# A recurrence with a gated MLP: a chunk's scaled keys loaded as two transfers of 416 KB instead of one of 832 KB, under a new instruction order

## The chip, the cores and the metric

The kernel runs on one core of a Trainium2 chip. The metric is the device time of one execution in microseconds. Five engines take part: TensorE (PE) multiplies matrices, VectorE (DVE) and ScalarE (ACT) work on elements, GpSimd (POOL) only fills memory at the start, and SyncE (SP) issues the DMA transfers. Each engine runs its own list of instructions in order, and semaphores hold an instruction until what it needs is there.

## The reference

For 4 batches of 8 heads a state of 40 x 40 is carried over 768 time steps, and each step's output row goes through an MLP of 320 to 2048 to 320 features. All is float32.

```python
for t in range(S):                       # S = 768, D = 40
    y[:, :, t] = einsum('bhd,bhde->bhe', rt, state)
    Sa = einsum('bhde,bhe->bhd', state, at)
    state = state * wt[:, :, None, :] - einsum('bhd,bhe->bhde', Sa, bt) \
          + einsum('bhd,bhe->bhde', vt, kt)
x = y.transpose(0, 2, 1, 3).reshape(B * S, H * D)     # 3072 x 320
h = x @ w_in
sp = maximum(h, 0) + log1p(exp(-abs(h)))
out = (h * erf(sp)) @ w_out
```

## The kernel before

The 768 steps are cut into 12 segments of 64 steps (q), and each segment into two chunks of 32 steps (c = 0 and 1; c0 and c1 below), so there are 24 chunks. Within a chunk the steps are done at once by matrix products; from chunk to chunk the state MT is carried. For each segment the kernel does these stages:

- `prep` (L423): loads the decays of a segment (Pr, L429) and takes products along time by scans on DVE (L436, L440).
- `aphase` (L451), once per chunk: one DMA (L465) loads 104 x 2048 numbers, 832 KB, into one buffer `bk`. Its first half holds k and b (called bk), its second half a, laid out by diagonal blocks (called ab). DVE scales the second half (L466, "ab") and the first half (L468, "bk"). PE multiplies both (A, L473). Two DMAs copy the scaled ab to Zs (zs, L478). DVE masks A's result (Am, L484), and a DMA writes part of it to DRAM (AD, L486). PE transposes the scaled bk half (bT, L492). The buffer exists once, so the next chunk's load waits for all of these readers. In the very first segment c1 uses a part of the MLP's buffer (h) instead.
- `tphase` (L497), once per segment: DMAs bring A's blocks to Ti (L506) and Aw (L509), DVE solves 16 x 16 triangular blocks in 14 steps (L519, L520), DMAs write the result to DRAM (TD, L522) and read it back in another layout (Tb, L525), DVE transposes it (L528), and PE completes the inverse by two products (W and DAD, L538), with DVE adding the result (L545).
- `chain` (L547), once per chunk, in the order of the recurrence: the state is copied (zmm, L569), PE computes Z (L577) and U (L588), the rows of U are copied into Vu (zu, L598; four copies per chunk, each by ACT, DVE or an SP DMA), PE transposes (pmt L605, UT L614) and multiplies (PQ L624, MY L638 and L642), DVE updates the state (L645) and scales the outputs (L647). Its inputs are loaded by zv, vx, rt and rv (L559 to L564). At the end of a segment xw (L652) writes the rows to DRAM.
- The MLP of a segment: `load_x` (xr, L794), `mm1` (L816), the activation in `unit` (L831) and `post` (L854) with the second product (L877). Its matmuls have no part in the recurrence, so they fill PE between the small products of the chain. In the tables below an MLP group is one `mm1`, one `mm2` or one `mm2s` step, or one of the weight-preparation or warm-up products at the start.

The weights are loaded and split into two float32r parts in the first 130 us (`weights`, L706), beside 190 warm-up matmuls (L420).

All steps are put into a list with their readers and writers (`Plan.add`, L190). Two constants found by a search outside the kernel decide the order: `ORDER` (L15) lists the steps as they are emitted, and `ENGINES` has one letter per step for its engine (P, A, V, G, or S for a DMA issued by SP). `schedule` (L210) only reads them. Each engine runs its steps in that order. Every DMA of the program is issued by SP, in one queue.

Of the kernel before, what the change touches and what calls it, by code (L numbers as in the profile page):

```python
# [985 lines left out]
```

## Time and profile before

| what | value |
|---|---|
| median of 3 runs | 834.38 us (827.68 to 841.53) |
| profiled execution, its own time | 835.12 us |
| its span, first to last instruction | 833.3 us |
| PE, DVE, ACT busy | 729.1, 653.2, 539.4 us |
| mean granted clock of TensorE | 0.923 of full speed |
| bytes by DMA | 94.54 MB, mean 113 GB/s |
| loads of scaled keys | 24 of 832 KB each |

The span is the time from the program's first instruction to its last. Busy time of an engine leaves out waits and the issuing of DMAs. A name such as `bk<-in_kba_e` says that tile bk is written from tensor in_kba_e; `L466` is line 466 of the kernel. "issue" stands where the profile sees nothing that an engine waits for. PEld is PE's loading of weights, which runs beside its matmuls.

### The profile page before, as it was taken

To read this page: it belongs to the slowest core of one execution; us is meant where nothing else is said; L and a number is where in the kernel's file an instruction comes from. 1 tells how busy PE (TensorE), PEld (TensorE's weight loads), DVE (VectorE), ACT (ScalarE), POOL (GpSimd) and SP (SyncE) were. 2 spreads that over 40 slices of the span, in tenths; PEclk is the share of its full clock that TensorE was granted. 3 is DMA by queue.
4 is the path that set the end of the run, shared out by engine and by line. 5 is a ranking of instruction groups with operands and counts; after the bars stand their busy time and mean duration, and the time that the engine had idled before them with its cause. 6 is when DMAs were issued, how large, how long until landed. Compare 5 with 4: busy or idle time off the path is not lost.

```text
span 833.3 us, 31311 instructions
## 1 busy us (share of the span) xinstructions
PE 729.1 (87%) x13999; PEld 612.0 (73%) x13999; DVE 653.2 (78%) x1137; ACT 539.4 (65%) x759; POOL 4.1 (0%) x9
## 2 busy tenths in 40 slices
...
GB/s 188 217 246 148 139 185 86 89 125 134 147 105 113 124 80 113 124 105 134 160 43 133 169 62 93 151 60 109 153 78 101 115 95 124 96 74 52 32 16 20
DMA packets 173210, 94.54 MB, mean 113 GB/s; under 512 B 145708, under 2 KB 157356, under 8 KB 170572
## 3 DMA queue, kind: packets, MB, share of 16 engines
...
q8 instruction: 112, 1.84, 1.0%
...
## 4 chain that ended last, share of the span: by engine, by line
PE 43%; DVE 20%; DMA 16%; issue 11%; ACT 7%; SPq 3%; DVEq 0%; ACTq 0%
PE po L877 11%; PE ph L816 11%; PE pA L538 4%; PE my L638 3%; SPq L380 3%; PE pA L473 3%; PE my L588 2%; DMA vt<-in_rv_e 2%; PE pQ L624 2%; DVE tmp L519 2%; DVE Ti L520 2%; DMA Tb<-TD 2%; ACT r L824 2%; DMA h<-in_kba_e 2%; DMA xr<-xd 2%
## 5 line engine op out<-in xcount | busy, mean ns | idle before, releaser
L877 PE MATMUL po<-wo,h 128*128 128x320 f32 x384 | 131.0, 466 | 4.4 <-issue 3.6
L824 ACT ACTIVATE l<-l 128x1024 f32<-128x1024 f32 x96 | 99.2, 1056 | 16.4 <-DVE nd L847 15.8
L816 PE MATMUL ph<-xh,wih 128*128 128x256 f32 x384 | 92.3, 323 | 9.7 <-issue 6.6
L877 PEld LDWEIGHTS po<-wo,h 128*128 128x128 f32 x384 | 70.8, 202 | 22.3 <-issue 5.4
L816 PE MATMUL ph<-xh,wil 128*128 128x256 f32 x384 | 80.4, 292 | 0.0
L816 PE MATMUL ph<-xl,wih 128*128 128x256 f32 x384 | 80.3, 292 | 0.0
L816 PEld LDWEIGHTS ph<-xh,wih 128*128 128x128 f32 x384 | 64.3, 198 | 19.3 <-issue 8.3
L877 PE MATMUL po<-woh,gh 128*128 128x320 f32 x192 | 70.4, 367 | 0.4 <-ACT gh L374 0.3
L816 PEld LDWEIGHTS ph<-xh,wil 128*128 128x128 f32 x384 | 63.0, 201 | 2.8 <-issue 2.8
L877 PE MATMUL po<-woh,gl 128*128 128x320 f32 x192 | 61.6, 321 | 3.0 <-DVE gl L865 3.0
L374 ACT COPY Us<-my 128x320 f32<-128x320 f32 x23 | 9.8, 426 | 82.1 <-PE my L588 82.1
L816 PEld LDWEIGHTS ph<-xl,wih 128*128 128x128 f32 x384 | 62.8, 201 | 0.0
L816 PE MATMUL ph<-xl,wir 128*128 128x256 f32 x192 | 56.9, 296 | 5.3 <-issue 5.1
L877 PE MATMUL po<-wol,gh 128*128 128x320 f32 x192 | 61.2, 319 | 0.0
L847 DVE TENSOR_TENSOR nd<-l,r 128x1024 f32<-128x1024 f32 x48 | 58.4, 1216 | 2.5 <-ACT r L824 1.3
L858 DVE TENSOR_TENSOR l<-l,r 128x1024 f32<-128x1024 f32 x48 | 58.3, 1217 | 0.8 <-ACT l L824 0.4
L859 DVE SCALAR_TENSOR_TENSOR h<-l,h 128x1024 f32<-128x1024 f32 x48 | 58.4, 1219 | 0.6
L848 DVE SCALAR_TENSOR_TENSOR r<-nd,r 128x1024 f32<-128x1024 f32 x48 | 58.4, 1216 | 0.5
L816 PE MATMUL ph<-xh,wir 128*128 128x256 f32 x192 | 56.3, 293 | 0.3 <-DVE xh L376 0.2
L374 ACT COPY h<-ph 128x512 f32<-128x512 f32 x75 | 43.0, 582 | 17.5 <-PE ph L816 16.2
L638 PE MATMUL my<-Vu,sg 64*40 64x72 f32 x1536 | 47.5, 233 | 5.4 <-issue 1.3
L824 ACT ACTIVATE r<-l 128x1024 f32<-128x1024 f32 x48 | 49.3, 1053 | 4.4 <-DVE l L858 2.5
...
## 6 DMA issues: line engine op xcount, KB each, us to landing
...
Pr<-in_w_e SPq DMA_DIRECT2D x12, 422.9 KB
...
```

Of the source, the lines that this page charges most:

```text
L374: self.nc.scalar.copy(o, i)
L380: self.P.add(name, [("SP", ISSUE.get(name, 0.41))] + [("POOLQ", 1.0)] * (name in BULK), lambda e: q[e].dma_start(o(), i()), rd, wr, pr)
L473: nc.tensor.matmul(pa[i % 2 * 64:i % 2 * 64 + 64, i // 4, i // 2 % 2], bk[:, i].rearrange("p a b -> p (a b)"), ab[:, :, i], start=True, st ...
L538: nc.tensor.matmul(pw[js, i, ts], l[js, i], r[js, i, ts], start=True, stop=True)
L638: nc.tensor.matmul(my[h * 64:h * 64 + 40, x, j], sg[xs, g, j, h], vu[xs, g * HQ + j // 2 * 2 + h, j % 2], start=True, stop=False)
L816: nc.tensor.matmul(ph[:, j * 256:j * 256 + 256], a[:k, fs], b[:k], start=(m == 0), stop=(m == 7))
L824: self.P.add(name, "ACT", lambda e: nc.scalar.activation(out=o, in_=i, **kw), rd, wr + ["act"], pr, 1.06)
L847: P.add("nd", [("DVE", 1.2)], lambda e, r=r, l=l, nd=nd: s.eng(e).tensor_tensor(out=nd, in0=l, in1=r, op=ALU.mult), kl + kr, kn, pr)
L848: P.add("rho", "DVE", lambda e, r=r, nd=nd: nc.vector.scalar_tensor_tensor(out=r, in0=nd, scalar=2 * C4, in1=r, op0=ALU.add, op1=ALU.mult) ...
L858: P.add("E", [("DVE", 1.2)], lambda e: s.eng(e).tensor_tensor(out=l, in0=l, in1=r, op=ALU.mult), kr, kl, pr)
L859: P.add("G", "DVE", lambda e: nc.vector.scalar_tensor_tensor(out=h, in0=l, scalar=-1.0, in1=h, op0=ALU.add, op1=ALU.mult), kl, kh, pr, 1.2)
L877: nc.tensor.matmul(po, y[:, bs], w, start=(f == 0 and m == 0), stop=(f == 15 and m == len(ops) - 1))
```

## The change

The single load of a chunk becomes two: first the second half of the buffer (ab), whose readers are `ab`, A and zs, and then the first half (bk), whose readers are `bk`, A and bT. Each has its own dependences, so each can be issued when its own half is free. Bytes, multiplies and products are as before.

```diff
-        s.dma("kba", lambda: kb, lambda: s.I["kba_e"][ck], wr=kk + ka, pr=pr)
+        hw = 2 * NP * 32
+        s.dma("kba", lambda: kb[:, hw:], lambda: s.I["kba_e"][ck][:, hw:], wr=ka, pr=pr)
+        s.dma("kba", lambda: kb[:, :hw], lambda: s.I["kba_e"][ck][:, :hw], wr=kk, pr=pr)
```

`ORDER` and `ENGINES` are replaced as a whole (3720 steps instead of 3696). All five lists change. What the two constants say, counted:

| step | before | after |
|---|---|---|
| loads of scaled keys, by SP | 24 | 48 |
| zu: ACT / DVE / SP | 46 / 30 / 20 | 50 / 41 / 5 |
| zt: ACT / DVE | 21 / 3 | 16 / 8 |
| xh: ACT / DVE | 21 / 15 | 15 / 21 |
| ghi: ACT / DVE | 15 / 9 | 10 / 14 |
| hc: ACT / DVE | 75 / 21 | 80 / 16 |
| Wm: ACT / DVE | 8 / 4 | 10 / 2 |
| bTc, ysM, vtu, ob, wlo, ohi: ACT / DVE | 142 / 31 | 133 / 40 |
| MLP groups on PE between the last W and the first DAD | 42 | 26 |
| MLP groups between U and UT | 21 | 17 |
| MLP groups between UT and PQ | 20 | 15 |
| MLP groups between PQ and MY | 15 | 19 |
| next segment's c0 load in SP's list, 10 steady segments: before TD / between TD and tb / after tb | 3 / 0 / 7 loads | 13 / 5 / 2 halves |
| c1 halves that stand next to each other in SP's list | | 5 of 11 |

Four fills of the start (zmm's buffer, MT and two others) also change engine. SP's list of one steady segment, from the solve's input to the chain's loads, before and after (kba.ab and kba.bk are the halves):

```
Ti Ti out xr xr out zv vx xr xr w Ap rt Ap vx TD TD zv tb tb rv kba zs zs rv rv kba
Ti Ti Ap xr out xr out zs Ap xr xr w out kba.ab zv rv TD TD kba.bk tb tb rv vx zs zs vx rt out kba.ab rv rv kba.bk
```

## Rows read from the trace of the kernel before

**Rows 1.** Head of the page and busy time: us, share of the span, instructions.
```profile
span 833.3 us, 31311 instructions
...
PE 729.1 (87%) x13999; PEld 612.0 (73%) x13999; DVE 653.2 (78%) x1137; ACT 539.4 (65%) x759; POOL 4.1 (0%) x9
```

**Rows 2.** The chain that ended last: shares of the span by engine.
```profile
PE 43%; DVE 20%; DMA 16%; issue 11%; ACT 7%; SPq 3%; DVEq 0%; ACTq 0%
```

**Rows 3.** PE's waits: us in total, times, longest us.
```profile
PE my L588 <- issue: 17.2, 7, 4.0
PE ph L816 <- issue: 11.7, 4, 6.6
PE pA L538 <- issue: 9.0, 6, 3.0
PE my L577 <- issue: 7.6, 3, 5.1
PE pA L538 <- DVE Ti L528: 6.3, 5, 2.0
```

**Rows 4.** DMA queues: packets, MB, share of 16 engines' span.
```profile
q8 instruction: 112, 1.84, 1.0%
```

**Rows 5.** PE in order of time: start, us, what, idle before it.
```profile
82.39 0.87 PE L588 MATMUL my<-zt,Tb 32*32 32x40 f32 x37 [3.88 <-issue]
...
314.52 0.78 PE L577 MATMUL my<-Zm,Zs 96*32 96x40 f32 x62
320.37 0.29 PE L577 MATMUL my<-Zm,Zs 96*32 96x40 f32 x2 [5.07 <-issue]
...
632.91 0.94 PE L588 MATMUL my<-zt,Tb 32*32 32x40 f32 x51 [3.30 <-issue]
```

**Rows 6.** SP in order of time: a c1 load's issue.
```profile
311.29 0.34 SPq L380 DMA_DIRECT2D bk<-in_kba_e  x1
```

**Rows 7.** DMA queues in two stretches: 311 to 317 us, then 317.4 to 319.
```profile
q1 hardware_dynamic: 498, 1.17, 84.1%
...
q8 instruction: 1, 0.02, 5.6%
```

**Rows 8.** DVE's waits for the loads: us, times, longest.
```profile
DVE bk L466 <- DMA bk<-in_kba_e: 5.3, 4, 1.8
...
DVE bk L468 <- DMA bk<-in_kba_e: 4.5, 3, 2.7
```

**Rows 9.** Issues of the load by SP: ns min/median/max, first and last start.
```profile
L380 SPq DMA_DIRECT2D bk<-in_kba_e x23: 318/337/2345, 2.6 to 690.5; - x23
```

**Rows 10.** The chain in order of time: start, us, what (a DMA: issue to landing).
```profile
276.82 4.07 DMA Pr<-in_w_e
...
373.23 7.21 DMA bk<-in_kba_e
...
526.61 5.85 DMA Pr<-in_w_e
...
696.58 2.94 DMA Vu<-Us
```

**Rows 11.** SP in order of time around TD and Tb, in two segments.
```profile
349.37 1.13 SPq L380 DMA_DIRECT2D TD<-Ti  x2
...
352.35 1.35 SPq L380 DMA_DIRECT2D Tb<-TD  x2
...
399.97 0.34 SPq L380 DMA_DIRECT2D bk<-in_kba_e  x1
...
405.19 1.13 SPq L380 DMA_DIRECT2D TD<-Ti  x2
...
411.93 1.34 SPq L380 DMA_DIRECT2D Tb<-TD  x2
```

**Rows 12.** Copies of U's rows (L598) as instructions: ns min/median/max.
```profile
L598 ACT COPY Vu<-Us x46: 453/457/461, 66.7 to 760.7; 32x320 f32<-32x320 f32 x46
L598 DVE COPY Vu<-Us x30: 316/320/325, 69.4 to 742.4; 32x320 f32<-32x320 f32 x30
```

More of the change, by code (lines that the diff above doesn't have):

```diff
@@ L15 @@
 ORDER = tuple(int(x) for x in """
[117 rows of a table removed]
[117 rows of a table added]
 """.split())
 ENGINES = "".join("""
-SSVVGVGGVAVAGGVVVAAPPPPPPPPPPPPPPPPPPPPPPPPPPPPPPPPPPPPPPPPPPPPPPPPPPPPPPPPPPPPPPPPPPPPPPPPPPPPPPPPPPPPPPPPPPPPPPPPPPPPPPPPPPPPPPPPPPPPPPPPPPPPPPPPPPP
-PPPPPPPPPPPPPPPPPPPPPPPPPPPPPPPPPPPPPPPPPPPPPPPPPPPPPPPPPPPSAVVVVSVVPPSSVVSSPAPASVVPPSSVVSSPAPASSSSAAVVVVVVVVVVVVVVVVVVVVVVVVVVVVSSSSVPPPPAPPPPVSVVVAP
-APASVVVAPAPASVVVAAAPAAPAVSVVVAPVPASVVVAPAPASVVVAAAPAAPAASVVVAPAPASVVVAPAPVSVVVAPAPASVVVAPAPASVVVAVSVVVAVSVVVVVSVVVAVSVVVAVSVVVSVVVSVVVSVVVSVVVSAVVVVSV
@@ L138 @@
-VPPSSVVSSPAPASSSSSSVAPPAPPAVAVVPAPVPAPPVPVVPVVSVVPPSSVVSSPAPASSSSSSAAPPAPPAAAVVPAPAPAPPVPVVPVVSSSSSSSSSSSSAAVVVVVVVVVVVVVVVVVVVVVVVVVVVVSSSSVPPPPVPPPP
-VSAVSAVSSAVPPAPPAAPPAPPAAAAAAAAAAVVVVAAAPPAPPAAPPVPPVAVVAVPPPPPPPPVVPPPPPPPPSAVVVVSVVPPSSVVSSPVPASSSSSSVAAPPVPPAAVAAPAPAPAPPVPVVPVVSVVPPSSVVSSPAPASSSS
-SSVAPPAPPAAVVVPAPAPVPPVPVVPVVSSSSSSSSSSSSAAVVVVVVVVVVVVVVVVVVVVVVVVVVVVSSSSVPPPPAPPPPVSAVSAVSSAVAAAAAAAAVVVVAAAPPAPPAAPPAPPAAVVAVPPPPPPPPVVPPPPPPPPASS
-ASSAAAAAAAAVVVVAAAPPAPPAAPPAPPAAVVAVPPPPPPPPVVPPPPPPPPSAVVVVSVVPPSSVVSSPAPASSSSSSVAAPPAPPAVAAVPAPVPVPPVPVVPVVSVVPPSSVVSSPVPASSSSSSVAPPAPPVAVVAPAPAPAPP
@@ L142 @@
-VPVVPVVSSSSSSSSSSSSAAVVVVVVVVVVVVVVVVVVVVVVVVVVVVSSSSVPPPPAPPPPVSAVSAVSSVVAAAAAAAAVVVVAAAPPAPPAAPPAPPAAVVVVPPPPPPPPVVPPPPPPPPASSVSSAAAAAAAAVVVVAAAPPAP
-PAAPPAPPAAVVAVPPPPPPPPVVPPPPPPPPSAVVVVSVVPPSSVVSSPAPASSSSSSVAAPPAPPAAAVAPAPVPAPPVPVVPVVSVVPPSSVVSSPVPASSSSSSVVPPAPPAVVVVPAPAPAPPVPVVPVVSSSSSSSSSSSSAAV
-VVVVVVVVVVVVVVVVVVVVVVVVVVVSSSSVPPPPAPPPPVSAVSVVSSVVAAAAAAAAVVVVAAAPPVPPAAPPAPPAAVVVVPPPPPPPPVVPPPPPPPPASSASSAAAAAAAAVVVVAAAPPAPPVAPPAPPAAVVVVPPPPPPPP
-VVPPPPPPPPSAVVVVSVVPPSSVVSSPVPASSSSSSVVVPPAPPAAAAAPAPAPAPPVPVVPVVSVVPPSSVVSSPAPASSSSSSVVPPAPPAAASSPAPVPAPPVPVVPVVSSSSSSSSSSSSAAVVVVVVVVVVVVVVVVVVVVVVV
@@ L146 @@
-VVVVVSSSSVPPPPAPPPPVSVVSAVSSVVAAAAAAAAVVVVAAAPPVPPAAPPAPPAAVVAVPPPPPPPPVVPPPPPPPPASSASSAAAAAAAAVVVVAAAPPAPPAAPPAPPAAVVAVPPPPPPPPVVPPPPPPPPSAVVVVSVVPPS
-SVVSSPAPASSSSSSVAAPPAPPAVAAAPAPVPAPPVPVVPVVSVVPPSSVVSSPAPASSSSSSAVPPAPPAAVVVPAPVPAPPVPVVPVVSSSSSSSSSSSSAAVVVVVVVVVVVVVVVVVVVVVVVVVVVVSSSSVPPPPAPPPPVSV
-VSAVSSVVAAAAAAAAVVVVAAAPPAPPAAPPAPPAAVVVVPPPPPPPPVVPPPPPPPPASSASSAAAAAAAAVVVVAAAPPVPPAAPPAPPAAVVAVPPPPPPPPVVPPPPPPPPSAVVVVSVVPPSSVVSSPAPVSSSSSSVAAPPAP
-PASSAAPAPAPAPPVPVVPVVSVVPPSSVVSSPAPVSSSSSSVVPPAPPAASSAPAPAPAPPVPVVPVVSSSSSSSSSSSSAAVVVVVVVVVVVVVVVVVVVVVVVVVVVVSSSSVPPPPVPPPPVSVVSAVSSAVAAAAAAAAVVVVAA
@@ L150 @@
-APPVPPAAPPAPPVAVVAVPPPPPPPPVVPPPPPPPPASSASSAAAAAAAAVVVVAAAPPAPPVAPPAPPAAVVAVPPPPPPPPVVPPPPPPPPSAVVVVSVVPPSSVVSSPAPVSSSSSSVAAPPVPPAAAASPAPAPAPPVPVVPVVS
-VVPPSSVVSSPAPASSSSSSVAPPAPPAVSVSPVPVPAPPVPVVPVVSSSSSSSSSSSSAAVVVVVVVVVVVVVVVVVVVVVVVVVVVVSSSSVPPPPAPPPPVSVVSAVSSVVAAAAAAAAVVVVAAAPPAPPAAPPAPPAAVVAVPPP
-PPPPPVVPPPPPPPPASSASSAAAAAAAAVVVVAAAPPAPPVAPPAPPAAVVAVPPPPPPPPVVPPPPPPPPSAVVVVSVVPPSSVVSSPVPASSSSSSVAAPPAPPASAAVPAPAPAPPVPVVPVVSVVPPSSVVSSPAPASSSSSSVV
-PPAPPAVAAVPAPAPAPPVPVVPVVSSSSSSSSSSSSAAVVVVVVVVVVVVVVVVVVVVVVVVVVVVSSSSVPPPPVPPPPVSAVSAVSSAVAAAAAAAAVVVVAAAPPVPPAAPPAPPAAVVAVPPPPPPPPVVPPPPPPPPASSASSA
@@ L154 @@
-AAAAAAAVVVVAAAPPVPPVAPPAPPAAVVVVPPPPPPPPVVPPPPPPPPSAVVVVSVVPPSSVVSSPAPVSSSSSSVAAPPAPPASAAAPVPAPAPPVPVVPVVSVVPPSSVVSSPAPASSSSSSAVPPAPPASSVVPVPVPAPPVPVV
-PVVSSSSSSSSSSSSAAVVVVVVVVVVVVVVVVVVVVVVVVVVVVSSSSVPPPPAPPPPVSAVSAVSSVVAAAAAAAAVVVVAAAPPVPPAAPPAPPAAVVAVPPPPPPPPVVPPPPPPPPASSASSAAAAAAAAVVVVAAAPPAPPAAP
-PAPPAAVVAVPPPPPPPPVVPPPPPPPPSAVVVVSVVPPSSVVSSPAPASSSSSSVAAPPAPPASAASPAPAPAPPVPVVPVVSVVPPSSVVSSPAPVSSSSSSVAPPAPPAAASSPAPVPAPPVPVVPVVSSSSSSSSSSSSAAVVVVV
-VVVVVVVVVVVVVVVVVVVVVVVSSSSVPPPPVPPPPVSVVSAVSSVVAAAAAAAAVVVVAAAPPVPPAAPPAPPAAVVVVPPPPPPPPVVPPPPPPPPASSASSAAAAAAAAVVVVAAAPPAPPAAPPAPPAAVVVVPPPPPPPPVVPP
@@ L158 @@
-PPPPPPSSSSSSVAVPPVPPAVSSSPAPAPAPPVPVVPVVSSSSSSVVPPAPPAAAAAPAPAPAPPVPVVPVVSSSSSSSSVPVVSVVSAVSSVVAAAAAAAAVVVVAAAPPVPPAAPPAPPVAVVVVPPPPPPPPVVPPPPPPPPVSSV
-SSAAAAAAAAVVVVAAAPPVPPVAPPVPPVAVVVVPPPPPPPPVVPPPPPPPPAAAAAAAAVVVVAAAVVAVPPPPPPPPVVPPPPPPPPASSASS
+SSVVGVGAGVGGAGVVGAAPPPPPPPPPPPPPPPPPPPPPPPPPPPPPPPPPPPPPPPPPPPPPPPPPPPPPPPPPPPPPPPPPPPPPPPPPPPPPPPPPPPPPPPPPPPPPPPPPPPPPPPPPPPPPPPPPPPPPPPPPPPPPPPPPPP
+PPPPPPPPPPPPPPPPPPPPPPPPPPPPPPPPPPPPPPPPPPPPPPPPPPPPPPPPPPPSAVVVVSSVVPPSSVVSSPAPASSVVPPSSVVSSPAPVSSSSAAVVVVVVVVVVVVVVVVVVVVVVVVVVVVSSSSVPPPPAPPPPVSVVV
@@ new lines @@
+APAPASVVVAPAPASVVVAAAPAAPAASVVVAPVPASVVVAPAPASVVVAAAPVVPAVSVVVAPAPASVVVAPAPASVVVAPVPASVVVAPVPASVVVVVSVVVVVSVVVAVSVVVAVSVVVAVSVVVSVVVSVVVSVVVSVVVSAVVVV
+SSVVPPSSVVSSPAPASSSSSSVAPPAPPAVAVVPAPAPAPPVPVVPVVSSVVPPSSVVSSPAPASSSSSSAVPPAPPAVAAVPVPAPAPPVPVVPVVSSSSSSSSSSSSAAVVVVVVVVVVVVVVVVVVVVVVVVVVVVSSSSVPPPPA
+PPPPVSAVSAVSSVVPPAPPAAPPAPPAAAAAAAAAAVVVVAAAPPVPPAAPPAPPAAVVVVPPPPPPPPVVPPPPPPPPSAVVVVSSVVPPSSVVSSPAPASSSSSSVAAPPAPPAAAVAPAPVPAPPVPVVPVVSSVVPPSSVVSSPA
+PASSSSSSAVPPAPPAVVVVPAPAPVPPVPVVPVVSSSSSSSSSSSSAAVVVVVVVVVVVVVVVVVVVVVVVVVVVVSSSSVPPPPAPPPPVSAVSAVSSVVAAAAAAAAVVVVAAAPPAPPAAPPAPPAAVVAVPPPPPPPPVVPPPPP
@@ new lines @@
+PPPASSASSAAAAAAAAVVVVAAAPPAPPAAPPVPPAAVVAVPPPPPPPPVVPPPPPPPPSAVVVVSSVVPPSSVVSSPVPASSSSSSVAAPPAPPAVAVAPAPVPAPPVPVVPVVSSVVPPSSVVSSPAPASSSSSSAVPPAPPAAAAA
+PVPAPAPPVPVVPVVSSSSSSSSSSSSAAVVVVVVVVVVVVVVVVVVVVVVVVVVVVSSSSVPPPPVPPPPVSAVSAVSSVVAAAAAAAAVVVVAAAPPAPPVAPPAPPAAVVVVPPPPPPPPVVPPPPPPPPASSASSAAAAAAAAVVV
+VAAAPPAPPVAPPAPPAAVVAVPPPPPPPPVVPPPPPPPPSAVVVVSSVVPPSSVVSSPAPVSSSSSSVAAPPVPPAAVAVPAPVPAPPVPVVPVVSSVVPPSSVVSSPAPASSSSSSVAPPAPPAVVVVPAPAPAPPVPVVPVVSSSSS
+SSSSSSSAAVVVVVVVVVVVVVVVVVVVVVVVVVVVVSSSSVPPPPAPPPPVSAVSVVSSVVAAAAAAAAVVVVAAAPPVPPVAPPAPPAAVVVVPPPPPPPPVVPPPPPPPPASSASSAAAAAAAAVVVVAAAPPAPPAAPPAPPAAVV
@@ new lines @@
+AVPPPPPPPPVVPPPPPPPPSAVVVVSSVVPPSSVVSSPAPVSSSSSSVVAPPAPPAAAAAPAPAPAPPVPVVPVVSSVVPPSSVVSSPAPASSSSSSVVPPAPPAAVVVPAPAPAPPVPVVPVVSSSSSSSSSSSSAAVVVVVVVVVVV
+VVVVVVVVVVVVVVVVVSSSSVPPPPAPPPPVSVVSAVSSVVAAAAAAAAVVVVAAAPPVPPAAPPAPPAAVVAVPPPPPPPPVVPPPPPPPPASSASSAAAAAAAAVVVVAAAPPAPPAAPPAPPAAVVAVPPPPPPPPVVPPPPPPPP
+SAVVVVSSVVPPSSVVSSPVPVSSSSSSVVVPPAPPAVVAVPVPVPAPPVPVVPVVSSVVPPSSVVSSPAPASSSSSSAAPPVPPAAAASPVPAPAPPVPVVPVVSSSSSSSSSSSSAAVVVVVVVVVVVVVVVVVVVVVVVVVVVVSSS
+SVPPPPAPPPPVSVVSAVSSVVAAAAAAAAVVVVAAAPPAPPAAPPAPPAAVVVVPPPPPPPPVVPPPPPPPPASSASSAAAAAAAAVVVVAAAPPAPPAAPPAPPAAVVAVPPPPPPPPVVPPPPPPPPSAVVVVSSVVPPSSVVSSPV
@@ new lines @@
+PASSSSSSVVAPPAPPAAVAVPAPAPAPPVPVVPVVSSVVPPSSVVSSPAPASSSSSSVAPPAPPASAVAPVPAPAPPVPVVPVVSSSSSSSSSSSSAAVVVVVVVVVVVVVVVVVVVVVVVVVVVVSSSSVPPPPVPPPPVSVVSAVSS
+VVAAAAAAAAVVVVAAAPPAPPVAPPAPPAAVVVVPPPPPPPPVVPPPPPPPPASSVSSAAAAAAAAVVVVAAAPPAPPAAPPAPPAAVVVVPPPPPPPPVVPPPPPPPPSAVVVVSSVVPPSSVVSSPAPVSSSSSSVVAPPVPPAVVA
+APAPAPAPPVPVVPVVSSVVPPSSVVSSPAPASSSSSSVVPPVPPAAASAPAPAPAPPVPVVPVVSSSSSSSSSSSSAAVVVVVVVVVVVVVVVVVVVVVVVVVVVVSSSSVPPPPAPPPPVSAVSVVSSVVAAAAAAAAVVVVAAAPPA
+PPAAPPAPPAAVVVVPPPPPPPPVVPPPPPPPPASSASSAAAAAAAAVVVVAAAPPAPPAAPPAPPAAVVVVPPPPPPPPVVPPPPPPPPSAVVVVSSVVPPSSVVSSPVPASSSSSSVAAPPAPPAAVVAPAPVPAPPVPVVPVVSSVV
```

7 lines of the change are left out of this document (added), and 234 rows, old and new, of the table ORDER.

## Prediction

> **What bounds the kernel now.** I read the head of the profile, the chain that ended last, the waits of TensorE (PE), the DMA queues, and then single stretches in order of time. The head shows a span of 833.3 us with PE busy 729.1 us, VectorE (DVE) 653.2 and ScalarE (ACT) 539.4 [rows 1]: PE is the busiest and stands idle for 104.2 us. The chain lies on PE for 43% of the span and for 11% on "issue", waits whose cause the profile does not name [rows 2]. The waits of PE show where: four groups released by "issue" hold 17.2 + 11.7 + 9.0 + 7.6 = 45.5 us [rows 3], nearly half of its idle time.
>
> What that is, the queues tell. Queue q8 carries 112 blocks of instructions, 1.84 MB [rows 4]; PE runs 2 x 13999 instructions [rows 1], so about 250 to a block (an estimate by division). In the stretch 310 to 324 us PE stops two matmuls before the end of a run of Z and goes on after 5.07 us [rows 5]. The load of a chunk's scaled keys, 832 KB, was issued at 311.3 us [rows 6]. From 311 to 317 us the one program queue q1 moves 498 packets and q8 none; from 317.4 to 319 us q8's block comes [rows 7], and PE resumes at 320.37. So PE runs out of code, and the next block stands behind the big load. Ten waits of PE of over 2 us ended by "issue" begin within 9 us of such a load's issue. By the time at which PE resumes they are 82.39 (3.88 us), 139.78 (4.54), 254.22 (2.27), 296.64 (6.63), 320.37 (5.07), 481.29 (2.69), 504.62 (3.30), 545.48 (2.33), 571.65 (3.96) and 632.91 (3.30), 38.0 us in all; the first, the fifth and the last are shown [rows 5]. Seven of the ten follow the load of a segment's second chunk (c1, 26.3 us), three that of a first chunk (c0, 11.7 us). DVE itself waits for these loads only 5.3 + 4.5 us [rows 8].
>
> **The change, part by part.** *Two halves instead of one load.* The multiplies, matmuls and copies stay; 24 issues become 48. An issue holds SP for 0.337 us [rows 9], so 8.1 us are added. Fifteen of the 20 copies of U rows (zu) that SP issued go to DVE (11) and ACT (4), so SP nets nothing; its spare time hides the rest. Each half has its own wait: the a·P half (ab) for the matmul A and the zs copies that read it, the k,b half (bk) for the transposes bT. Behind a half that waits stand TD, tb, zs and rv on SP, and the solve's matmuls W and the Z and PQ of the chain wait for those.
>
> *Code held behind the load.* A load of 832 KB takes 7.21 us from issue to landing. The nearest row for 416 KB is Pr, 422.9 KB in as many rows: 4.07 and 5.85 us [rows 10]. A block of code can so be held 1.4 to 3.1 us less; between ends not far apart I take the middle, 2.25. For c1, seven waits, each longer than that: 7 x 2.25 = 15.8 us. Ends: 0, if both halves hold code like one load (5 of the 11 c1 pairs stand next to each other in SP's list), and 21.1 with 3.1 each (the 2.27 wait cannot give more). The Trainium skill, DMA: Bandwidth & Descriptors, section "Queues, rings and completion order", says that a DMA engine takes turns between queue rows packet by packet; by that adjacent halves, too, hold a block for one half only, and the sum would stay 15.8 without the end at 0. That a block comes while a big load's packets are done and later ones still flow [rows 7] agrees, but no row shows two loads together.
>
> *The c0 load moves.* In the steady segments the old order issued 3 of 10 c0 loads before TD (the solve's write), 7 after tb (its read-back). The new list has 13 of 20 halves before TD, 5 between TD and tb, 2 after. Before TD, PE runs MLP matmuls, and none of the three old loads there (one stands in [rows 11]) is followed by a wait for code within 9 us. I take 13/20 of the c0 waits as gone: 11.7 x 13/20 = 7.6 us; ends 0 and 11.7.
>
> Together 23.4 us of PE's idle time. How much reaches the end? The chain runs over PE and its issue waits for 43% + 11% [rows 2]; where PE is released earlier elsewhere, DVE (78% busy) or a DMA is late next. I take 0.55: 12.9 us; ends 0 and 32.8 (21.1 + 11.7, all of it).
>
> *The solve's round trip.* This is what the move costs. Normally TD's issue to Tb's takes 352.35 - 349.37 = 2.98 us; in the segment where the load went out 5.2 us before TD it took 411.93 - 405.19 = 6.74 [rows 11], 3.76 more. For five halves between TD and tb I take half of that, 1.9 us, and that it shows in 5 of 12 segments, since W already waits for the transposed block Ti five times in 12 segments [rows 3]: 5 x 1.9 x 5/12 = 4.0 us lost. Ends 0 and 18.8.
>
> *zu off SP.* One such copy by DMA lies on the chain with 2.94 us [rows 10]; as an instruction it takes 0.32 on DVE or 0.457 on ACT [rows 12]. One of the fifteen on the path gains 2.5 us, which I take; ends -3.5 (11 x 0.32 on DVE, none on the path) and 15 x 2.5 = 37.5, far too much, as the chain shows one. DVE has 180 us free to hide the new copies; without that cover they cost the 3.5.
>
> *The rest of the order.* PE's list has the same instructions. MLP groups between W and DAD fall from 42 to 26 (12 segments), between U and UT from 21 to 17, UT and PQ from 20 to 15; between PQ and MY they rise from 15 to 19. Some 30 other small instructions change between ACT and DVE both ways, under DVE's spare time. PE's idle time beside the four groups is 58.7 us; I take 0, ends 10 us (a sixth of that) either way.
>
> The sum: 12.9 + 2.5 - 4.0 = 11.4 us. The profiled execution took 835.1 us (span and 1.8 us around it), 0.7 above the median of the runs, 834.4. 835.1 - 11.4 - 0.7 = 823.0.
>
> **Rivals.** *Code is held as before* (the halves stand in the rings as one load; what is gained at one block is lost at another, as 112 blocks meet 48 loads). For it: rv pairs and other loads stand around the c1 load. Against: c0 loads before TD left no wait. Only zu and the round trip remain: 834.4 - 2.5 + 4.0 = 836. The Trainium skill, Runtime: NRT & Kernel Launch, section "Instruction fetch mechanics", calls the cost of a block boundary mostly hidden; by that there would be nothing to gain, and the time is this rival's. The waits of 3 to 6 us here [rows 5] disagree; the measurement decides.
>
> *Slower: the round trip becomes the bound.* Loads before and between TD and tb make Tb late in all ten steady segments by the whole 3.76 us of [rows 11], 37.6 us. It decides from the point where the MLP groups ahead of W are used up, so that PE waits for Ti each time. Less the gains above (15.4): 834.4 + 37.6 - 15.4 = 857. For it: 18 of 20 halves are now ahead of tb. Against: in 7 of 12 segments W does not wait for Ti today, and a half is in flight a shorter time.
>
> *Much faster: code waits behind key loads vanish.* If a block held by a half always comes before PE's stored code ends, all 38.0 us go, and reach the end, with zu's 2.5: 834.4 - 40.5 = 794; with the round trip's price 798. For it: waits of 2.3 to 3.3 us (five of ten) are about as long as what a half saves. Against: DVE and ACT then bound stretches.
>
> **How the numbers follow.** Forecast 0.48 (own range 812 to 834: half the way to each term's end, added in squares), code held as before 0.22, slower 0.12, much faster 0.18. Two per cent is about what a measurement of this kernel tells from no change: below 817.7 or above 851.1. Faster: nearly all of the last case (0.17), a third of the forecast (0.16) and a hundredth of the second, 0.34; slower: 0.10 of the slower case and 0.02 from elsewhere, 0.12; within, 0.54. The range takes in part of both outer cases: 802 to 842.
>
> **What would show it.** Right: issue waits of PE over 2 us within 9 us of a key load fall from 38.0 to about 15 us, none longer than 4.5; PE busy stays near 729; two issues per chunk on SP; TD to Tb around 3 to 5 us. The code part is wrong if those waits still sum to over 30 us; the round-trip term if Tb follows TD by 6 us in most segments and W's wait for Ti is above 20 us in total; the order if PE's idle time grows outside both.

## The result, and the profile after

The changed kernel takes 785.29 us (median of 4 runs, 782.47 to 789.87), the kernel before 837.95 in the runs beside it (4 runs, 827.68 to 842.34): a ratio of 0.9455 [0.9353, 0.9557], faster by 5.5%. Medians are of all runs and ratios of the runs near each kernel's fastest, so a ratio is not the quotient of two medians. The forecast was 823.0 with a range of 802 to 842; the time lies outside the range and below even the rival called much faster (794).

The head of the page of the changed kernel, busy time, and the shares of its chain, as in [rows 1, 2]:

```profile
span 780.7 us, 31363 instructions
...
PE 710.6 (91%) x13999; PEld 597.3 (77%) x13999; DVE 658.7 (84%) x1164; ACT 534.7 (68%) x748; POOL 4.6 (1%) x11
...
PE 52%; DVE 28%; issue 7%; ACT 6%; DMA 5%; SPq 1%; DVEq 0%; ACTq 0%
```

The span is 52.6 us shorter, and that comes in two pieces. PE's idle time (span less busy) falls from 104.2 to 70.1 us, by 34.1. PE's busy time falls from 729.1 to 710.6, by 18.5, with the same 13999 matmuls. On the chain, DMA falls from 16% to 5% and issue from 11% to 7%; PE and DVE take their place.

PE's waits that "issue" ended (lines after the load stand two further down: L588 of [rows 3] is L590, L816 is L818, L538 is L540, L577 is L579):

```profile
PE pA L540 <- issue: 10.3, 13, 1.8
PE my L579 <- issue: 3.2, 3, 2.8
PE ph L818 <- issue: 3.1, 2, 2.0
PE pA L540 <- DVE Ti L530: 1.9, 4, 0.9
PE my L590 <- issue: 0.7, 2, 0.5
```

The four groups of [rows 3] held 45.5 us; they hold 17.3. The one that remains, at L540, is 13 short waits, none over 1.8 us (9.0 us before, 10.3 now). The wait of the solve's matmul for Ti (DVE) fell from 6.3 to 1.9. Added up over the trace, PE's waits over 0.25 us that "issue" ended and that begin within 9 us of the issue of a key load ("near waits" from here on) were 41.4 us before and are 10.4 now. Of the ten over 2 us, 38.0 us in all, one of 2.80 is left. VectorE (DVE) waited 12.1 us for the key loads (the two groups of [rows 8] and 2.3 us for the first tile's load); now no wait of DVE is ended by one.

How a block of code comes through is seen in the queues, two stretches of the changed kernel around a c1 pair whose halves were issued at 290.89 and 295.84 us: first 290.9 to 294.7, then 294.5 to 296.

```profile
q1 hardware_dynamic: 617, 0.49, 46.7%
...
q1 hardware_dynamic: 87, 0.01, 5.6%
q8 instruction: 1, 0.02, 4.2%
```

In the first stretch q1 moves 0.49 MB, the first half among it, and q8 nothing; in the second q1 is nearly empty and q8's block comes (294.78 to 295.79), just before the second half is issued. PE does not wait for this block. The block of [rows 7] came when 93 of the load's 104 packets had ended. The chain shows the length of one half, issue to landing (start, us, what):

```profile
582.03 3.63 DMA bk<-in_kba_e
```

That is 3.63 us against 7.21 for the whole load [rows 10]. These are single rows: over all loads, from the issue to the end of the last packet, the median is 6.7 us for the 24 whole loads before and 3.9 us for the 48 halves.

The issues themselves cost what [rows 9] said (ns min/median/max), and a Tb behind a half that was issued between TD and Tb comes 4.36 us after TD (SP in order of time, as [rows 11]):

```profile
L380 SPq DMA_DIRECT2D bk<-in_kba_e x46: 308/338/1732, 1.3 to 642.9; - x46
```

```profile
328.49 1.15 SPq L380 DMA_DIRECT2D TD<-Ti  x2
329.73 0.51 SPq L380 DMA_DIRECT2D bk<-in_kba_e  x1
332.85 1.36 SPq L380 DMA_DIRECT2D Tb<-TD  x2
```

**Where the busy time went.** The page's costliest group did the same 384 matmuls in less time, first before, then after (busy us, mean ns of one):

```profile
L877 PE MATMUL po<-wo,h 128*128 128x320 f32 x384 | 131.0, 466 | 4.4 <-issue 3.6
```

```profile
L879 PE MATMUL po<-wo,h 128*128 128x320 f32 x384 | 124.6, 446 | 0.2 <-DVE h L861 0.2
```

The mean granted clock was 0.923 before and is 0.959 after. Windows of the kernel before around the fifth wait of [rows 5] show when it falls (us, busy of PE, PEld, DVE, ACT, POOL, then PEclk, DMA share, GB/s):

```profile
300.00:315.30 15.30, 15.11 (x495) 12.81 (x495) 11.26 (x16) 8.64 (x14) 0.00 (x0) 0.93 0.27 64
315.30:320.40 5.10, 0.03 (x2) 0.03 (x1) 1.42 (x2) 0.00 (x0) 0.00 (x0) 0.88 0.86 185
320.40:326.10 5.70, 5.70 (x83) 4.98 (x82) 3.09 (x4) 3.14 (x6) 0.00 (x0) 0.51 0.16 29
326.10:340.00 13.90, 13.86 (x251) 11.96 (x251) 12.33 (x16) 9.55 (x13) 0.00 (x0) 1.00 0.46 111
```

PE waits 5.07 us for its code, and the 5.70 us of work behind it run at 0.51, which is the 1.2 GHz level; then the clock is back at 2.4 GHz. So this wait is paid twice. Time at the lower level was 130.5 us before and is 66.4 after. All ten waits of the prediction, and an eleventh of 1.81 us near a key load, have such a stretch that begins inside the wait or within 1 us of its end. These eleven stretches are 81.9 of the 130.5 us; in the changed kernel 3.4 of the 66.4 us stand so behind a near wait, and the other 63.0 do not.

### The profile page after: what moved, and what is told of

The parts are those of the page before. It is cut to its first block, busy times and chain, and to the rows that moved or that the text cites. A ratio compares the mean times of both kernels' runs of the same rounds, so it can differ in the third digit from the quotient of the medians.

```text
span 780.7 us, 31363 instructions
## 1 busy us (share of the span) xinstructions
PE 710.6 (91%) x13999; PEld 597.3 (77%) x13999; DVE 658.7 (84%) x1164; ACT 534.7 (68%) x748; POOL 4.6 (1%) x11
## 4 chain that ended last, share of the span: by engine, by line
PE 52%; DVE 28%; issue 7%; ACT 6%; DMA 5%; SPq 1%; DVEq 0%; ACTq 0%
PE ph L818 14%; PE po L879 13%; PE ph L420 5%; PE pA L540 4%; PE my L640 3%; DVE Zs L486 2%; DVE h L861 2%; PE pA L475 2%; DVE l L860 2%; DVE r L850 2%; DMA TD<-Ti 2%; DVE Ti L522 2%; DVE gl L867 2%; DVE tmp L521 2%; DMA Tb<-TD 2%
## 5 line engine op out<-in xcount | busy, mean ns | idle before, releaser
L879 PE MATMUL po<-wo,h 128*128 128x320 f32 x384 | 124.6, 446 | 0.2 <-DVE h L861 0.2
L818 PE MATMUL ph<-xh,wih 128*128 128x256 f32 x384 | 92.1, 321 | 1.1 <-issue 1.1
L818 PE MATMUL ph<-xl,wih 128*128 128x256 f32 x384 | 79.9, 290 | 2.3 <-issue 2.0
L879 PEld LDWEIGHTS po<-wo,h 128*128 128x128 f32 x384 | 67.5, 192 | 16.6 <-DVE h L861 0.5
L818 PE MATMUL ph<-xh,wil 128*128 128x256 f32 x384 | 79.4, 290 | 0.0
L879 PE MATMUL po<-woh,gh 128*128 128x320 f32 x192 | 73.1, 380 | 4.4 <-DVE ob L376 3.7
L818 PEld LDWEIGHTS ph<-xh,wih 128*128 128x128 f32 x384 | 63.3, 195 | 6.8
L374 ACT COPY h<-ph 128x512 f32<-128x512 f32 x80 | 46.7, 584 | 30.6 <-PE ph L818 24.9
L818 PEld LDWEIGHTS ph<-xl,wih 128*128 128x128 f32 x384 | 61.8, 198 | 2.7 <-issue 2.3
L818 PEld LDWEIGHTS ph<-xh,wil 128*128 128x128 f32 x384 | 62.2, 199 | 0.0
L818 PE MATMUL ph<-xh,wir 128*128 128x256 f32 x192 | 55.6, 289 | 2.6 <-DVE xh L376 2.6
L640 PEld LDWEIGHTS my<-Vu,sg 64*40 64x40 f32 x1536 | 36.4, 117 | 26.2 <-DVE Vu L629 10.9
L818 PE MATMUL ph<-xl,wir 128*128 128x256 f32 x192 | 55.8, 291 | 0.1
L420 PE MATMUL ph<-d 104*128 104x512 bf16 x190 | 50.4, 405 | 1.6 <-DVE d L391 1.6
```

The source lines that it names most:

```text
L374: self.nc.scalar.copy(o, i)
L420: P.add("warm", "PE", lambda e: nc.tensor.matmul(s.ph[1], s.d1[:, :128], s.d1[:, :512], start=True, stop=True), ["d1"], ["phw"], -1e3, 0.22)
L640: nc.tensor.matmul(my[h * 64:h * 64 + 40, x, j], sg[xs, g, j, h], vu[xs, g * HQ + j // 2 * 2 + h, j % 2], start=True, stop=False)
L818: nc.tensor.matmul(ph[:, j * 256:j * 256 + 256], a[:k, fs], b[:k], start=(m == 0), stop=(m == 7))
L879: nc.tensor.matmul(po, y[:, bs], w, start=(f == 0 and m == 0), stop=(f == 15 and m == len(ops) - 1))
```

## The experiments

Each ratio is to the kernel before in runs on the same chip. "Old order" and "changed order" name the lists of steps and engines of the two kernels.

**1. Halves or order?** Three kernels complete a table. Old order, the halves next to each other where the one load stood:

```diff
-s.dma("kba", lambda: kb, lambda: s.I["kba_e"][ck], wr=kk + ka, pr=pr)
+s.dma("kba", lambda: kb[:, hw:], lambda: s.I["kba_e"][ck][:, hw:], wr=ka, pr=pr)
+s.dma("kba", lambda: kb[:, :hw], lambda: s.I["kba_e"][ck][:, :hw], wr=kk, pr=pr)
 ORDER: each load's number becomes two, next to each other
```

> The order and engines of the kernel before, with each load cut into its two halves, issued next to each other where the one load stood. Theory H (blocks of code are held behind a key load, a half holds them for half as long, adjacent halves let a block in between): waits of PE on issue within 9 us of a key load fall from 41 us to 10 to 18, the granted clock rises above 0.94, time 795 to 815 us. Theory O (the gain is the new order's; loads are placed and products covered better): waits on issue stay near 40 us, time 830 to 840 us.

Changed order, one load, at the place of the later half; four ab multiplies that would come before it move behind it:

```diff
-s.dma("kba", lambda: kb[:, hw:], lambda: s.I["kba_e"][ck][:, hw:], wr=ka, pr=pr)
-s.dma("kba", lambda: kb[:, :hw], lambda: s.I["kba_e"][ck][:, :hw], wr=kk, pr=pr)
+s.dma("kba", lambda: kb, lambda: s.I["kba_e"][ck], wr=kk + ka, pr=pr)
```

> The new order and engines, but one load of 832 KB, at the place of the later of its two halves (four multiplies of ab move behind it). Theory H: waits on issue within 9 us of a key load come back to 25 to 40 us, clock near 0.93, time 815 to 835 us. Theory O: time 785 to 800 us, waits on issue below 15 us.

Changed order, both halves next to each other at that same place:

```diff
 ORDER, every chunk
-ab half, other steps, bk half
+other steps, ab half, bk half
```

> The changed kernel with both halves of a load issued next to each other, at the place of the later one; the same as the new order with one load (841 us) except that the load is in two. Theory H (a half holds code for half as long wherever it stands): 785 to 800 us, waits on issue near loads 10 to 20 us. Theory P (the earlier place of the first half matters, not the halving): 825 to 845 us, waits on issue near loads over 30 us.

Measured: old order in halves 811.17 us, 0.9743 [0.9645, 0.984]; changed order with one load 840.92, 1.0127 [1.0033, 1.0221]; with adjacent halves 818.21, 0.9809 [0.9737, 0.9881]. So halving in place gives 2.6% in the old order and 3.1% in the new, and the new order with one load gives nothing, or costs a little. The rest of the 5.5%, from 0.9809 to 0.9455, comes with the earlier place of the first half. What the order costs with one load is seen in DVE's waits for it, 32.2 us, with single waits over 6 us:

```profile
DVE bk L466 <- DMA bk<-in_kba_e: 19.6, 9, 6.3
...
DVE bk L468 <- DMA bk<-in_kba_e: 12.6, 3, 7.6
```

**2. Which chunk's early half?** Changed kernel, adjacent halves for the first chunks (c0) only, then for the second chunks (c1) only:

```diff
 ORDER, every first chunk
-ab half, other steps, bk half
+other steps, ab half, bk half
```

> Changed kernel (785 us), but the two halves of every first chunk (c0) are issued together, at the place of the later one; the second chunk's (c1) stay apart. With both chunks together it took 818 us, so 33 us are to be shared out. If the early half counts by the prediction's terms (c1 15.8, c0 7.6), about two thirds of the 33 us stay: 796 us (790 to 802), with the waits over 2 us near key loads at 8 to 10 us (4.8 with both apart, 17.2 with both together). If c0's early half is what counts, because DVE multiplies sooner and the transfers of TD are not behind 832 KB: 808 to 818 us. If a single early half is worth nothing without the other: 812 to 820 us.

```diff
 ORDER, every second chunk
-ab half, other steps, bk half
+other steps, ab half, bk half
```

> Changed kernel, but the two halves of every second chunk (c1) are issued together, at the place of the later one, with the few multiplies that then come too early moved behind; the first chunk's (c0) stay apart. By the prediction's terms c1 carries two thirds of the 33 us: 807 us (800 to 812), waits over 2 us near key loads 12 to 15 us. If c0's early half is what counts: 787 to 796 us. If neither is worth anything alone: 812 to 820 us.

(The 4.8 and 17.2 us in these texts count every issue wait over 2 us; in the changed kernel one of its two, of 2.05 us, begins 9.6 us after a load.) Measured: c0 together 804.76 us, 0.9682 [0.9622, 0.9742]; c1 together 790.38, 0.9528 [0.951, 0.9547]. These times stand beside other runs of the kernel before than those of e7 and of the changed kernel, so the ratios are to be compared: 0.9809 with both together, 0.9455 with both apart. C1's early halves alone bring 1.3% (some 11 us), and their interval touches that of both together; c0's alone bring 2.8% (some 23 us), and their interval lies inside that of the changed kernel. So c0's early half carries most of it, and no share of c1's is clear of noise. The traces agree: near waits are 20.7 us with c0 together and 9.6 with c1 together. Two lines of the kernel with c0 together, PE's wait and DVE's, show the largest part:

```profile
PE pA L540 <- issue: 18.9, 12, 7.2
```

```profile
DVE bk L470 <- DMA bk<-in_kba_e: 12.9, 2, 6.8
```

The 7.2 and the 6.8 us stand behind one c0 pair, issued 4.4 and 6.0 us after TD; the other wait of DVE, 6.1 us, is for the program's first loads.

**3. The copies of U rows.** Changed kernel with the engines of these copies (zu) as before, 20 on SP; old order with 18 of the 20 taken off SP, in one load and in halves; changed kernel with the last five on DVE:

```diff
 ENGINES, zu
-5 S
+20 S
```

> The changed kernel, with only the engines of the copies of U's rows (zu) as before: 20 of them by SP again instead of 5. The prediction's term: 2.5 us lost, so 787 to 789 us. If each of the fifteen lay on the path: up to 822 us. If the copies had no part: 783 to 787 us.

```diff
 ENGINES, zu, old order, one load
-20 S
+2 S, 7 more V, 11 more A
```

> The kernel before, one load and the old order, with 18 of the 20 copies of U's rows (zu) that SP issued given to the engines that the changed kernel uses (DVE 7, ACT 11). Theory Q (a zu issue at the head of SP's queue waits for U, and holds every transfer behind it): PE's waits other than issue fall by 10 us or more, time 805 to 820 us where before has 829. Theory of the prediction (one of the copies is on the path): 2 to 3 us less, 826.

```diff
 ENGINES, zu, old order, adjacent halves
-20 S
+2 S, 7 more V, 11 more A
```

> The old order with both: halves next to each other (811 us alone, as measured) and the 18 zu copies off SP. If the two parts add up and Q holds: 790 to 805 us, and the new order has little left to give over this. If the new order is what makes them work: 806 to 812 us.

```diff
 ENGINES, zu
-5 S
+0 S, 5 more V
```

> The changed kernel with the last five zu copies off SP as well (to DVE). Theory Q: 3 to 10 us less, 775 to 782 us. If only a crowd of such copies holds SP: no difference, 783 to 787 us.

Measured, in this order: 822.35 us, 1.0001 [0.9958, 1.0044]; 847.06, 1.0164 [1.01, 1.0228]; 822.92, 0.9874 [0.9805, 0.9944]; 788.96, 0.9481 [0.9421, 0.9541]. In the old order the move costs 1.3 to 1.6%; in the changed order taking it back costs all, or nearly all, that the change won, although near waits stay low there (6.6 us). The last five copies make no difference clear of noise. In the kernel with 20 copies on SP, PE waits for loads that stand behind the copies in SP's list:

```profile
PE my L640 <- DMA Vu<-in_v_x: 9.5, 6, 3.4
...
PE my L640 <- DMA AD<-Zs: 5.1, 1, 5.1
PE my L644 <- DMA Rt<-in_r_e: 4.2, 2, 2.1
```

None of these three is among PE's waits in the changed kernel. PE's busy time is up as well, to 729.8 us, with 121.3 us at the lower clock level:

```profile
span 822.1 us, 31379 instructions
...
PE 729.8 (89%) x13999; PEld 613.5 (75%) x13999; DVE 656.0 (80%) x1153; ACT 532.8 (65%) x744; POOL 4.6 (1%) x11
```

Against the changed kernel that is 22.2 us more idle and 19.2 us more busy time of PE. None of those slow stretches begins in or within 1 us behind a near wait: other waits have them too. So the changed order works only with the copies' new engines, and this term has no worth by itself.

**4. Size of a transfer, or length of its packets?** The halves are smaller transfers, and their packets are 4 KB instead of 8. One load with a gap of 64 B in the middle of each row, so that it moves in 4 KB packets; then gaps in DRAM that make 2 KB packets:

```diff
+two = restride(kb[:, :2 * hw].rearrange("p (x n) -> p x n", x=2), 1, hw + gap)
-s.dma("kba", lambda: kb, lambda: s.I["kba_e"][ck], wr=kk + ka, pr=pr)
+s.dma("kba", lambda: two, lambda: s.I["kba_e"][ck].rearrange("p (x n) -> p x n", x=2), wr=kk + ka, pr=pr)
```

> The kernel before, with 64 bytes left free in SBUF between the two halves of the buffer, so that the one load of 832 KB is made of runs of 4 KB, 16 to a DMA engine, instead of 8 of 8 KB. If a block of code is held for the whole transfer that stands ahead of it (theory H as stated): nothing changes, waits on issue near 40 us, time 828 to 842 us. If it is held by the length of a run alone, or by a fixed number of runs: waits on issue fall to 10 to 20 us and the time to 795 to 815 us.

```diff
-s.dma("kba", lambda: kb, lambda: s.I["kba_e"][ck], wr=kk + ka, pr=pr)
+s.dma("kba", lambda: kb.rearrange("p (x n) -> p x n", x=4), lambda: s.I["kba_e"][ck].rearrange("p (x n) -> p x n", x=4)[:, :, :NP * 32], wr=kk + ka, pr=pr)
```

> Kernel before, its order, one transfer of 832 KB per chunk, but its rows in DRAM stand in four pieces of 2 KB with 64 B of nothing between, so that it moves in packets of 2 KB as the four transfers of 208 KB do. In four transfers it took 788 us (ratio 0.950); one transfer in rows of 4 KB took as long as before (0.9965). If the length of the packets is what lets a code block through: 785 to 800 us, waits over 2 us near key loads about 13 us. If it is the number of transfers (the pause on SP and between one transfer and the next): 823 to 832 us, ratio 0.99 to 1.00, waits near key loads 25 to 41 us.

Measured: 828.85 us, 0.9965 [0.992, 1.001], and 828.72, 1.0005 [0.9965, 1.0045]: no gain. Yet the near waits fell, to 27.0 and 16.7 us. In their place DVE waits for the load, 27.0 us with 2 KB packets:

```profile
DVE bk L467 <- DMA bk<-in_kba_e: 13.8, 6, 3.9
...
DVE bk L469 <- DMA bk<-in_kba_e: 10.9, 7, 2.7
```

SP needs longer to issue such a load, 0.872 us against 0.337 [rows 9], and as long with 4 KB packets (median 0.872):

```profile
L381 SPq DMA_DIRECT2D bk<-in_kba_e x23: 840/872/2692, 2.6 to 678.0; - x23
```

Both waits count, then. Old order, four and eight transfers next to each other, by columns, each multiply waiting for its own half's parts (parts is 2, then 4, and 1 in the first segment's c1); four by partitions, so that packets stay at 8 KB and each multiply needs all four; and the halves in 2 KB packets:

```diff
+for lo, keys in ((hw, ka), (0, kk)):
+    for x in range(parts):
+        xs = slice(lo + x * hw // parts, lo + (x + 1) * hw // parts)
+        s.dma("kba", lambda xs=xs: kb[:, xs], lambda xs=xs: s.I["kba_e"][ck][:, xs], wr=keys if parts == 1 else [keys[x]], pr=pr)
```

> Kernel before, its order and its engines, the load in four transfers of 208 KB next to each other instead of one of 832 KB (of the first tile's second chunk in two). In halves it took 811 us (ratio 0.974). If what counts is the size of one transfer, another step of the same kind: 795 to 805 us, waits over 2 us near key loads from 32 to about 20 us, near ones in all from 33 to about 24. If what counts is how many bytes are asked for at one time, the same as in halves: 806 to 816 us, ratio 0.97 to 0.98. If three more issues of 0.32 to 0.6 us each on SP delay the transfers behind them: 815 to 825 us.

> Kernel before, its order, the load in eight transfers of 104 KB next to each other. One, two and four took 830, 811 and 788 us; waits near key loads were 41, 33 and 25 us. If each halving takes another step off: 770 to 780 us. If the end is near, because the code waits left have other causes and SP's issues (eight of 0.3 to 0.6 us, 3 to 4 us for a chunk) hold back the transfers behind them: 785 to 800 us. Central guess 786 us.

```diff
+for x in range(4):
+    rows = slice(x * 32, min(x * 32 + 32, 104))
+    s.dma("kba", lambda rows=rows: kb[rows], lambda rows=rows: s.I["kba_e"][ck][rows], wr=[kk[x], ka[x]], pr=pr)
```

> Kernel before, its order, the load in four transfers next to each other by partitions (32, 32, 32 and 8 rows of 8 KB), so the packets stay at 8 KB and each multiply needs all four, as before. One transfer in 8 KB or 2 KB packets took 829 us, four by columns in 2 KB packets 788. If the number of transfers alone does it: 785 to 800 us, waits near key loads about 25 us. If it needs short packets as well, so that a code block comes through early while the four are issued: 815 to 830 us, waits near key loads 33 to 41 us. In between, 800 to 815 us, both count. Central guess 808 us.

```diff
+four = lambda t: t.rearrange("p (x n) -> p x n", x=4)
+s.dma("kba", lambda: four(kb)[:, 2:], lambda: four(s.I["kba_e"][ck])[:, 2:, :NP * 32], wr=ka, pr=pr)
+s.dma("kba", lambda: four(kb)[:, :2], lambda: four(s.I["kba_e"][ck])[:, :2, :NP * 32], wr=kk, pr=pr)
```

> Kernel before, its order, the load in two transfers of 416 KB next to each other as in e1 (811 us), but in packets of 2 KB by gaps in DRAM. If the number of transfers alone counts: 806 to 816 us. If packets count once the load is in several transfers: 792 to 804 us, waits near key loads 20 to 27 us. If the cut rows make the load late, as with one transfer (SP's issue 0.95 us instead of 0.48, DVE's waits for the load 25 us instead of 10): 815 to 828 us. Central guess 810 us.

The same loop in the changed order, in four and in eight transfers:

> Changed kernel, each half in two transfers of 208 KB (of the first tile's second chunk not). Code waits over 2 us near key loads are 4.8 us in all there, so by size of transfer at most 5 to 8 us are left to win: 777 to 783 us. If bytes at one time count: the same, 783 to 790 us. If the 46 further issues on SP, 0.32 to 0.6 us each, push back the transfers on the chain: 790 to 798 us.

> Changed kernel, each half in four transfers of 104 KB. With whole halves 785 us, in halves of these 773 us; waits near key loads 10 us in both. If smaller transfers go on helping: 762 to 769 us. If SP's issues now hold back the chain's transfers: 775 to 785 us. Central guess 774 us.

All kernels of the four experiments in one table; near waits, DVE's waits for the key load and the time at the 1.2 GHz level are added up from one profiled execution each, the ratios from several runs:

| kernel | transfers, packets | near waits us | DVE waits us | us at 1.2 GHz | ratio |
|---|---|---|---|---|---|
| before | 1, 8 KB | 41.4 | 12.1 | 130.5 | 1 |
| e5, zu off SP | 1, 8 KB | 45.6 | 14.8 | 114.8 | 1.0164 [1.01, 1.0228] |
| e4 | 1, 4 KB | 27.0 | 29.0 | 126.8 | 0.9965 [0.992, 1.001] |
| e13 | 1, 2 KB | 16.7 | 27.0 | 110.4 | 1.0005 [0.9965, 1.0045] |
| e1 | 2, 4 KB | 33.3 | 5.2 | 100.8 | 0.9743 [0.9645, 0.984] |
| e6, zu off SP | 2, 4 KB | 28.8 | 2.7 | 110.6 | 0.9874 [0.9805, 0.9944] |
| e17 | 2, 2 KB | 31.5 | 3.3 | 100.7 | 0.9708 [0.9631, 0.9785] |
| e16 | 4 by rows, 8 KB | 24.7 | 14.0 | 83.7 | 0.9653 [0.9578, 0.9729] |
| e11 | 4, 2 KB | 24.6 | 3.9 | 64.2 | 0.9503 [0.9478, 0.9528] |
| e14 | 8, 1 KB | 11.8 | 3.0 | 45.8 | 0.9376 [0.9329, 0.9424] |
| changed order, one (e2) | 1, 8 KB | 35.4 | 32.2 | 133.3 | 1.0127 [1.0033, 1.0221] |
| changed order, adjacent (e7) | 2, 4 KB | 20.1 | 12.3 | 106.9 | 0.9809 [0.9737, 0.9881] |
| c0 together (e9) | 2, 4 KB | 20.7 | 12.9 | 93.0 | 0.9682 [0.9622, 0.9742] |
| c1 together (e10) | 2, 4 KB | 9.6 | 0.6 | 90.9 | 0.9528 [0.951, 0.9547] |
| 20 zu on SP (e3) | 2 apart, 4 KB | 6.6 | 6.1 | 121.3 | 1.0001 [0.9958, 1.0044] |
| no zu on SP (e8) | 2 apart, 4 KB | 9.2 | 0 | 54.9 | 0.9481 [0.9421, 0.9541] |
| changed kernel | 2 apart, 4 KB | 10.4 | 0 | 66.4 | 0.9455 [0.9353, 0.9557] |
| changed order (e12) | 4, 2 KB | 10.8 | 0.3 | 51.6 | 0.9329 [0.9303, 0.9355] |
| changed order (e15) | 8, 1 KB | 7.9 | 0.2 | 45.4 | 0.9304 [0.923, 0.9379] |

(e13's profiled execution, 822 us, was the fastest of its ten, which ran to 836, so its waits are low for its ratio.) In the old order, then, the number of transfers decides the time: two in 4 or 2 KB packets take the same, and four in 8 KB packets are much faster than one in 2 KB. Shorter packets of one transfer do let code through sooner (41.4, 27.0, 16.7 us of near waits), but DVE then waits longer for the load. Between e16 and e11 the ratio falls from 0.9653 to 0.9503; these two differ in the separate waits of the multiplies and in packets, so neither's share is shown. Quartered in place, with nothing else changed, the old kernel is as fast as the changed one within the intervals; in eighths it takes 776.61 us. In the old order, from one transfer to eight, PE's busy time falls from 729.1 to 700.0 us:

```profile
span 777.7 us, 31642 instructions
...
PE 700.0 (90%) x13999; PEld 588.2 (76%) x13999; DVE 652.8 (84%) x1137; ACT 538.9 (69%) x759; POOL 4.1 (1%) x9
```

The changed order in quarters takes 772.77 us (772.41 to 775.67), in eighths 767.25 (763.75 to 775.36): both clearly faster than the kernel before. Their ratios lie below that of the changed kernel, but the intervals touch it and each other. In eighths the changed order's head and busy time read:

```profile
span 762.0 us, 31656 instructions
...
PE 700.5 (92%) x13999; PEld 588.9 (77%) x13999; DVE 659.3 (87%) x1164; ACT 534.6 (70%) x748; POOL 4.6 (1%) x11
```

## Why the prediction was wrong

The sum gave 11.4 us, and the span fell by 52.6. Three steps failed: PE's busy time was held to stay near 729 us (18.5 us missed), a share of 0.55 was taken of the code waits (the idle time fell in full), and the code term itself was too small (23.4 us against 31.0). Near waits counted at 31.0 us instead of 12.9, and busy time, make 36.6 of the 41.2 us by which the sum fell short; the other 4.6 are the rest of PE's idle time, down 3.1 us where zu and the round trip were to add 1.5.

**Right: where the time was.** PE's waits near key loads go with the size of the load, and the change took them away: 38.0 us over 2 us became 2.8. Issues cost nothing that shows (338 ns each), and the order with one load is worth little: e2 lost 1.3%, some 10 us, the end of the term's range. "Code held behind the load" is not the whole of it: before four of the eleven near waits the key load had ended, by 0.2 to 2.3 us, when the block began to move. In the longest of these gaps, before the wait that ends at 571.65 us, other loads of q1 kept the DMA engines 88% busy, so a block can stand behind these as well.

**Wrong: the size of a half.** "I take the middle, 2.25" per wait came from the w load's rows, 4.07 and 5.85 us. A half takes 3.63 us on the chain, 3.58 less than the 7.21; by the medians of all loads and halves it is 2.8 less, inside the 1.4 to 3.1 of the forecast. So the price of one wait was near, if low. What the term left out is the place: in the changed order halves next to each other took 15.3 us off the near waits (35.4 to 20.1) and the earlier place of one half another 9.7 (to 10.4). In the old order halves next to each other took off 8.1 (e1). The forecast took 23.4 us of the 38.0 away; near waits fell by 31.0.

**Wrong: c0 against c1.** The prediction gave c1 15.8 us and c0 7.6. The runs gave c1's early half 1.3% alone, some 11 us and not clear of noise, and c0's 2.8%, some 23 us (e9, e10); they measure the earlier place, not the halving. For c0 the prediction counted only the waits of PE that stood behind a c0 load in the old order. In the new order, with the halves of c0 together, PE at L540 waits 7.2 us once behind a pair and DVE 6.8 us for it; in the changed kernel both waits are gone.

**Wrong: the share of 0.55.** "Where PE is released earlier elsewhere, DVE or a DMA is late next" did not happen: PE's idle time fell by 34.1 us, as much as the near waits (31.0) and a little over, and in sum nothing of it came back as a wait for DVE or a DMA. That holds for this order and these engines, not in general: with 20 zu copies on SP (e3) near waits fell by 34.8 us and PE's idle time by only 11.9, because waits for other loads came in their place, and with one load in 2 KB packets (e13) by 24.7 and 8.5. DVE had its own wait for the load, 12.1 us, that went with the same halves. The prediction listed 5.3 + 4.5 of it as a sign that DVE was not held, and gave it no term.

**Missing: the clock.** "PE busy stays near 729" was wrong by 18.5 us, a third of the gain. The rows were there: [rows 1] give PE's busy time as if it were fixed work, and no window behind a wait of [rows 5] was read for its granted clock. In the old order, from one transfer to eight, PE's idle time fell by 26.4 us (104.2 to 77.8) and its busy time by 29.1 (729.1 to 700.0); time at the lower clock fell from 130.5 to 45.8 us. That the clock falls with waits of PE is read from the windows and from this table; no run changed the clock by itself. Near waits alone do not tell it: e3 has 6.6 us of them and 121.3 us at the lower level, e10 9.6 and 90.9.

**zu: right sign, wrong kind.** The term of 2.5 us treated the move as worth something by itself. It costs 1.3 to 1.6% in the old order and holds up the changed one (e3: ratio 1.0001 without it). A sum of parts cannot show this.

**Round trip: priced for nothing.** The 4.0 us lost, and the slower rival built on it, did not show. The price of 3.76 us came from one segment of [rows 11]; in the two others of the old order with a load 4.3 and 4.9 us before TD, Tb follows TD by 3.87 and 3.33 us, so the load was not shown to be what held it. Tb follows TD by 3.98 us in the mean of twelve segments (3.62 before), and still the solve's wait for Ti fell from 6.3 to 1.9 us. The sign named for this term, "W's wait for Ti" above 20 us, went the other way.

**The rivals.** "Code held as before" leaned on the Trainium skill, Runtime: NRT & Kernel Launch, section "Instruction fetch mechanics", by which crossing a block boundary is mostly hidden. Here that holds for the count and not for the cost: the trace has 14 near waits to 112 blocks, but they are 41.4 us, and cutting them gave 31.0 of the 52.6 us. From the Trainium skill, DMA: Bandwidth & Descriptors, section "Queues, rings and completion order" (each DMA engine takes turns between queue rows and drains a whole packet before it switches), the prediction drew that adjacent halves hold a block for one half only. In e1 near waits fell by 8.1 us, not by the 15.8 drawn from it, and in at least eight of the ten over 1.5 us more than 150 of the pair's 208 packets had ended before the block's packet began; so that conclusion is not borne out. The rival called much faster had the waits nearly right (all 38.0 us gone, 2.8 left) and its 794 us is the nearest; it, too, left out the clock.

**What stays open.** Why four transfers issued, in most chunks, within 2 us let code through and one transfer of the same bytes, even in short packets, does so only by making DVE late, the traces do not settle. SP's longer issue and the multiplies' waits have a part in it; how the queues share the engines among several transfers was not isolated. Two more rivals were not run: one load at the early place of the first half, and another order found for one load. So how much of the gain only the changed order can give is not settled, as the old order with the load in four comes as far.
